# Windowed attention and a gated feed-forward: q and k of two batches loaded with two neighbouring tokens in a partition, and sorted apart by VectorE ahead of the transposes

## The chip, the cores and the metric

The kernel runs on one core of a Trainium2 chip. TensorE (PE in the profile) multiplies matrices out of the on-chip memory SBUF into the accumulators (PSUM); VectorE (DVE) and ScalarE (ACT) work on elements and empty PSUM; GpSimd (POOL) and SyncE (SP) issue most of the DMAs that move data between the device's memory and SBUF. The metric is the device time of one execution in microseconds (us); lower is better.

## The reference

q, k and v have 4 batches, 8 heads, 768 tokens and a head size of 64. A query attends to the first 4 tokens (the sinks) and to itself and the 127 tokens before it. What comes out, with the heads side by side (3072 rows of 512), goes through a feed-forward without a nonlinearity:

```python
scores = scale * np.matmul(q, k.transpose(0, 1, 3, 2))
keep = is_sink | in_window            # pos < 4, or 0 <= rel < 128
scores = np.where(keep, scores, -1000000000.0)
a = np.exp(scores - np.max(scores, axis=-1, keepdims=True))
a = a / (np.sum(a, axis=-1, keepdims=True) + 1e-09)
attn = np.matmul(a, v)                # then (4*768, 512)
h = (attn @ w1) * (attn @ w2) @ w3    # w1, w2: 512x1024, w3: 1024x1024
out = h @ w_out                       # 1024x512, float32
```

## The kernel before

Everything is computed in bf16 with fp32 accumulation. The tokens of a batch are 6 blocks `kb` of 128, or 3 pairs `t` of blocks.

**Weights.** `w3 @ w_out` is folded into one matrix `w3o` once: w3 is transposed on TensorE in pieces (`fold_w3`, tiles `tp3`, L407, which VectorE copies to `w3t`, L412) and multiplied with `w_out` (`fold_mm`, tiles `ph` and `pw`, L437). Nine 512 KB pieces of w3 and `w_out` come as fp32 from SyncE (L165), are parked in tiles that are not yet used, among them q's and k's of batch 1 (`kN_88`, `qN_84`, `kqT_96`), and are cast by VectorE and ScalarE (L417). The rest comes from GpSimd's queue, whose DMAs cast on the way.

**Attention.** `load_qkv` (L108 to 110) loads, for a block of 128 tokens, k, q and v in one DMA each: partition p holds token p of the block, and each of its 8 heads is a run of 64 elements. `transposes` (L208 to 216) then makes eight 128x128 transposes of the block's k and q on TensorE (L213) into one PSUM tile `tp`, and one VectorE copy (L215) brings it to `kqT`, in which tokens run along the free dimension. Batch 2 and 3 have part of their transposes done by DMA from SyncE instead (`XPOSE`). Scores of k against q (`sc`, L260 and L281; of the sinks `sp`, L242), the exponential on ScalarE (`ex`, L265 and L285), the mask on VectorE (`am`, L269 and L289), the product with v (`av`, L313 and L350), and the division by the row's sum on VectorE (`rec` and `xn`) follow; `xn` is transposed into `xT`.

**Feed-forward.** `gate` (L383 to 399) multiplies `xT` with w1 and w2 (`pg`, L390); ScalarE empties the one (L397) and VectorE multiplies the other with it (`ab`, L394). `project` (L447 to 462) multiplies `ab` with `w3o` (`po`, L451), ScalarE empties it, and SyncE stores it.

**What sets the order.** Each piece of work is a `task` with a priority, a list of stages (engine and a planned duration), what it comes after, the loads it needs and the PSUM ring it takes a buffer from. `service` and `landings` (L474 to 514) plan when each load arrives, from `order`, the list of GpSimd's DMAs. `plan` (L674) goes through time by these figures and picks the next task of each engine; `nudge` adds to priorities and `PACE` sets least distances between score tasks. The outcome is one fixed order of instructions for each engine: at run time an engine takes its instructions in that order, and one that waits for a semaphore holds up all behind it. Where the plan sees TensorE idle early on, it puts in `keep_busy` multiplications (`pz`, L468) that nothing uses. The planned duration of a transposes task is 0.45 on TensorE and 0.65 on VectorE (L576).

Of the kernel before, what the change touches and what calls it, by code (L numbers as in the profile page):

```python
# [21 lines left out]
def kernel(  # L22
# [13 lines left out]
    nc = tc.nc  # L36
    FP32 = mybir.dt.float32
    BF16 = mybir.dt.bfloat16
# [19 lines left out]
    X_XPOSE = ((1, 0), (1, 1), (1, 2), (2, 0), (2, 1), (2, 2), (3, 0), (3, 1), (3, 2))  # L58
    HALVED = ((3, 1), (3, 2), (3, 3))
    SPLIT = 6  # L60
    scale = 1.0 / float(D) ** 0.5

    const = ctx.enter_context(tc.tile_pool(name="const", bufs=1))
# [2 lines left out]
    work = ctx.enter_context(tc.tile_pool(name="work", bufs=3))  # L66
# [4 lines left out]
    ident = const.tile([P, P], BF16, name="ident")  # L71
# [28 lines left out]
    def rows(src, b, kb):  # L100
        return src[b, :, kb * P:(kb + 1) * P, :].rearrange("h p d -> p h d")

    def heads(ap):
        return ap.rearrange("p (h d) -> p h d", d=D)

    kqv = k, q, v

    def load_qkv(b, kb):  # L108
        for src, dst in zip(kqv, (heads(kN[b][:, kb, :]), heads(qN[b][:, kb, :]), vN[b][:, kb, :, 0:D])):
            nc.gpsimd.dma_start(out=dst, in_=rows(src, b, kb))  # L110

# [17 lines left out]
    def load(what, *i):  # L129
# [9 lines left out]
        else:  # L139
            for dst, src in ((w1_sb, moe_w1), (w2_sb, moe_w2)):  # L140
# [5 lines left out]
            ("w3", 3, 4, "dve")]  # L146
    hold = 5

    order = [("w3", 6, 8), ("qkv", 0, 0, 1), ("qkv", 0, 1, 2), ("w3", 5, 6), ("qkv", 0, 2, 3),
             ("qkv", 0, 3, 4), ("w12", 0, 1), ("w12", 1, 2), ("w12", 2, 3), ("w12", 3, 4), ("qkv", 0, 4, 5),  # L150
             ("qkv", 0, 5, 6), ("qkv", 1, 0, 6), ("qkv", 2, 0, 6), ("qkv", 3, 0, 6)]

    nudge = {("g", 0, 1, 5, 0): -300, ("g", 1, 0, 6, 1): 60, ("p", 3, 5, 256): -300, ("g", 2, 0, 3, 0): -300}

    def flat(tile_, names):
        return tile_[:].rearrange(f"p {names} -> p ({names})")
# [47 lines left out]
    for x in order:  # L204
        if x[0] != "qkv" or x[1] == 0:
            load(*x)

    def transposes(b, kb):  # L208

        tp = ps_mm.tile([P, 2, NP, P], BF16, tag="mm", name="tp")  # L210
        for i, src in enumerate((kN[b], qN[b])):
            for r in range(NP):
                nc.tensor.transpose(tp[:, i, r, :], src[:, kb, r * P:(r + 1) * P], ident)  # L213
        yield
        nc.vector.tensor_copy(kqT[b][:, :, :, kb * P:(kb + 1) * P], tp[:])  # L215
        yield

    def transposes_dma(src, dst, kb):
# [254 lines left out]

    def service(what, *i):  # L474
        if what == "qkv":
            return [(0.95 if i[0] == 0 else 0.87, 0.845 if 6 * i[0] + kb < 14 else 2.1, [(x, i[0], kb)])
                    for kb in range(i[1], i[2]) for x in "kqv"]
# [85 lines left out]
    for b in range(B):  # L563
        for t in range(NT):
            kbs = (2 * t, 2 * t + 1)
            qk = []
            war = [("av", b - 2, NP - 1, NT - 1)] if b >= 2 else []
            for kb in kbs:
                if (b, t) in XPOSE:
                    for n, src, dst in (("k", kN[b], kT[b]), ("q", qN[b], qT[b])):  # L570
                        qk.append(("td" + n, b, kb))
                        task(qk[-1], 1, transposes_dma(src, dst, kb), [("sp", 1.4), ("dma", 1.2)],
                             war, [(n, b, kb)])
                else:
                    qk.append(("tpk", b, kb))
                    task(qk[-1], 1, transposes(b, kb), [("pe", 0.45), ("dve", 0.65)],  # L576
                         war, [("k", b, kb), ("q", b, kb)], "mm")
            if t == 0:
                task(("sk", b), 0, sink_keys(b), [("dve", 0.2)], [("sc", b, 1, 0)])
                task(("sv", b), 2, sink_values(b), [("dve", 0.6)],  # L580
                     [("av", b - 1, 1, NT - 1)] if b else [], [("vc",)])
            else:
                if b not in SINKS:
                    task(("ss", b, t), -1, sink_scores(b, t, t + 1), [("pe", 0.12), ("act", 0.4)],
                         qk + [("sk", b)], ring="mm", started=[] if (b, t) in BLOCKS else [("sc", b, 1, t)])
                elif t == 1:
                    more = [(n, b, kb) for n in (("tdk", "tdq") if (b, 2) in XPOSE else ("tpk",)) for kb in (4, 5)]
                    task(("ss", b, 1), -1, sink_scores(b, 1, NT), [("pe", 0.225), ("act", 0.6)],
                         qk + more + [("sk", b)], ring="mm", started=[("sc", b, 1, 1)])
            if (b, t) in BLOCKS:  # L590
                parts = [(j, r0, r0 + 2, [2 * i + r0 // 2]) for i, j in enumerate(kbs) for r0 in (0, 2)]
                if t == 0:
                    parts = [(0, 0, NP, [0, 1])] + parts[2:]
                for u, (j, r0, r1, avs) in enumerate(parts):
                    lead, more = j in PAIRS and r0 == 0, j in PAIRS and r0 > 0
                    task(("sc", b, u, t), 0 if more else 4, block_scores(b, j, r0, r1),
                         [("pe", 0.23), ("act", 1.05), ("dve", 0.7)],
                         [("tpk", b, kb) for kb in (j - 1, j) if kb >= 0], ring="sc",
                         slots=2 if lead else 1, paced=not more,
                         started=([unit[-1][0]] if unit else [])  # L600
                         + (unit[-3 if lead else -4][1] if len(unit) > 3 else []))
# [12 lines left out]
            for r in range(NP):  # L614
                after = list(qk)
                if b >= 2 and t == 0:
                    after += [("g", b - 2, len(CHUNKS[b - 2]) - 1, dt, 1) for dt in range(KFF)]
                lead = r % 2 == 0
                task(("sc", b, r, t), 4 if lead else 0, scores(b, r, t),
                     [("pe", 0.17), ("act", 0.83), ("dve", 0.58)] if t == 0 else  # L620
                     [("pe", 0.225), ("act", 1.05), ("dve", 0.7)], after, ring="sc",
                     slots=2 if lead else 1, paced=lead,
                     started=([unit[-1][0]] if unit else []) + (unit[-3][1] if lead and len(unit) > 3 else []))
                task(("av", b, r, t), 3, values(b, r, t),
                     [("pe", 0.187 if t == 0 else 0.36), ("dve", 0.55)],
                     [("sc", b, r, t)] + ([("ss", b, 1 if b in SINKS else t), ("sv", b)] if t else []),
                     [("v", b, kb) for kb in kbs], "mm", last_av)
                last_av = [("av", b, r, t)]
                unit.append((("sc", b, r, t), last_av))
                if not lead and (b, t) not in X_XPOSE:  # L630
                    task(("xt", b, r - 1, t), 2.5, x_transposes(b, r - 1, t),
                         [("pe", 0.225), ("act", 0.6)],
                         [("av", b, r - 1, t), ("av", b, r, t)], [], "mm")
            if (b, t) in X_XPOSE:
                for i in range(2):
                    task(("xd", b, t, i), 1, x_transposes_dma(b, t, i), [("sp", 1.3), ("dma", 1.2)],
                         [("av", b, NP - 1, t)])
    gates = []
    for b in range(B):
# [26 lines left out]
    MARGIN = {"av": 0.3}  # L666

    YIELD = {"g": 0.0, "av": 0.0, "sc": 0.4, "tdk": 1.5, "tdq": 1.5}
    PACE = [[0, 0, 0], [0, 0, 0], [0, 0, 7.6], [8.9, 3, 5.4]]
    TURN, SHAPE = 0.095, {"sc": 1, "ss": 2}  # L670
    START, WARM_UNTIL = 1.2, 40.0
    BACKLOG = 1.6
# [158 lines left out]
```

## Time and profile before

| | us |
|---|---|
| median of 3 runs (lowest, highest) | 195.99 (195.43, 197.69) |
| span of the profiled execution, from its first to its last instruction | 193.9 |
| TensorE busy in the span | 186.7 |
| VectorE busy in the span | 114.7 |
| ScalarE busy in the span | 103.0 |
| 12 VectorE copies `kqT<-tp` (L215) | 8.3 |
| 24 loads each of k, q and v, median from issue to landing | 8.2 to 8.6 |

The span is the one time that the profile has of its execution; the median of the runs, which were not profiled, is 2.1 us more, which holds what lies ahead of the first instruction and behind the last as well as the difference between executions.

How to read it: busy time counts from an instruction's start to its end, and TensorE overlaps its multiplications, so that the time from one start to the next is less than the duration in a row. In a timeline a row has the start, the time from the first start to the last end, the engine, the line, and in brackets the idle time of that engine ahead of it with what ended it. An engine that idles costs time only where the engine that sets the end waits for it.

### The profile page before, as it was taken

To read this page: it belongs to the slowest core of one execution; us is meant where nothing else is said; L and a number is where in the kernel's file an instruction comes from. 1 tells how busy PE (TensorE), PEld (TensorE's weight loads), DVE (VectorE), ACT (ScalarE), POOL (GpSimd) and SP (SyncE) were. 2 spreads that over 40 slices of the span, in tenths; PEclk is the share of its full clock that TensorE was granted. 3 is DMA by queue.
4 is the path that set the end of the run, shared out by engine and by line. 5 is a ranking of instruction groups with operands and counts; after the bars stand their busy time and mean duration, and the time that the engine had idled before them with its cause. 6 is when DMAs were issued, how large, how long until landed. Compare 5 with 4: busy or idle time off the path is not lost.

```text
span 193.9 us, 4599 instructions
## 1 busy us (share of the span) xinstructions
PE 186.7 (96%) x1808; PEld 123.1 (63%) x1825; DVE 114.7 (59%) x277; ACT 103.0 (53%) x175; POOL 75.2 (39%) x102
## 2 busy tenths in 40 slices
PE   7899999999999999999999999999999999999994
PEld 2344556898867787588799556654666565655542
DVE  5554687856699887678785435660588564444100
ACT  4052289743766876575764627352884563333232
POOL 5189987688899863443155351000000000000000
PEclk9999999999999999999999999999999999999999
DMA  6999999999999999999999999999320432000144
GB/s 219 372 391 179 170 159 196 196 161 153 155 147 194 195 150 119 154 133 238 144 140 158 144 164 209 190 153 205 113 52 6 110 110 55 0 0 3 68 162 149
DMA packets 108021, 29.17 MB, mean 150 GB/s; under 512 B 98656, under 2 KB 103904, under 8 KB 108000
## 3 DMA queue, kind: packets, MB, share of 16 engines
q0 software_dynamic: 79520, 12.33, 90.4%
q1 hardware_dynamic: 28336, 16.49, 40.5%
q8 instruction: 14, 0.23, 0.5%
q10 hardware_dynamic: 144, 0.07, 0.1%
q14 instruction: 7, 0.06, 0.1%
HBM read 29.39 MB, written 6.29 MB: 184 GB/s over the span
## 4 chain that ended last, share of the span: by engine, by line
PE 88%; DMA 8%; SPq 1%; issue 1%; DVE 0%; POOL 0%; ACT 0%
PE pg L390 44%; PE po L451 21%; PE av L350 7%; PE sc L260 5%; DMA ab<-in_moe_w_out_dram 4%; DMA w_sb<-in_moe_w_dram 4%; PE tp L213 3%; PE pw L437 3%; PE av L313 1%; PE sc L281 1%; PE tp L407 1%; PE ph L437 1%; SPq L165 1%; PE sp L242 1%; PE xt L329 1%
## 5 line engine op out<-in xcount | busy, mean ns | idle before, releaser
L390 PE MATMUL pg<-xT,w_sb 128*128 128x256 bf16 (+1 forms) x640 | 90.8, 294 | 0.0
L390 PEld LDWEIGHTS <-w_sb 128*128 128x128 bf16 x640 | 59.8, 98 | 20.7 <-issue 1.7
L397 ACT COPY a_sb<-pg 128x256 f32<-128x256 f32 (+1 forms) x80 | 33.3, 416 | 37.4 <-PE pg L390 24.1
L394 DVE TENSOR_TENSOR ab<-a_sb,pg 128x256 bf16<-128x256 f32 (+1 forms) x80 | 37.6, 471 | 23.8 <-PE pg L390 21.2
L451 PE MATMUL po<-w3o,ab 128*128 128x512 bf16 (+2 forms) x196 | 42.7, 362 | 0.5
L265 ACT ACTIVATE ex<-sc 128x1024 bf16<-128x1024 f32 (+1 forms) x40 | 37.9, 963 | 5.3 <-PE sc L260 4.6
L269 DVE TENSOR_TENSOR am<-ex,maskt 128x1024 bf16<-128x1024 bf16 (+1 forms) x40 | 25.3, 646 | 12.8 <-ACT ex L265 12.8
L451 PEld LDWEIGHTS <-ab 128*128 128x128 bf16 x208 | 19.1, 98 | 19.7 <-issue 0.2
L455 ACT COPY w_sb<-po 128x512 f32<-128x512 f32 (+2 forms) x25 | 14.1, 564 | 26.2 <-PE po L451 24.1
L110 POOL DMA_DIRECT2D kN<-in_k_dram x24 | 21.6, 900 | 13.1 <-DMA qN<-in_q_dram 9.2
L110 POOL DMA_DIRECT2D qN<-in_q_dram x24 | 21.8, 909 | 11.9 <-DMA vN<-in_v_dram 7.7
L110 POOL DMA_DIRECT2D vN<-in_v_dram x24 | 21.4, 893 | 8.6 <-DMA kN<-in_k_dram 7.6
L357 DVE TENSOR_TENSOR xn<-av,rec 128x256 bf16<-128x256 f32 x40 | 17.0, 425 | 1.4
L350 PE MATMUL av<-vN,am 128*128 128x65 bf16 x296 | 16.9, 193 | 0.0
L350 PEld LDWEIGHTS <-am 128*128 128x128 bf16 x296 | 14.5, 97 | 2.3 <-issue 0.2
L354 DVE RECIPROCAL rec<-av 128x4 f32<-128x4 f32 x40 | 7.2, 180 | 12.3 <-PE av L350 12.2
L260 PE MATMUL sc<-kqT 64*128 64x128 bf16 (+1 forms) x216 | 11.6, 238 | 0.1
L350 PE MATMUL av<-vs,es 128*128 128x130 bf16 x56 | 11.1, 221 | 0.0
L285 ACT ACTIVATE ex<-sc 128x1024 bf16<-128x1024 f32 x7 | 7.1, 1045 | 5.3 <-PE sc L281 5.3
L260 PEld LDWEIGHTS <-kqT 64*128 64x128 bf16 x216 | 6.9, 94 | 4.0 <-issue 3.4
L215 DVE COPY kqT<-tp 128x1024 bf16<-128x1024 bf16 x12 | 8.3, 689 | 1.8 <-PE tp L213 1.7
L437 PE MATMUL ph<-wo_sb,w3t 128*128 128x512 bf16 x32 | 8.1, 379 | 0.4 <-DVE w3t L412 0.3
(70 smaller groups left out, 126.5 us busy)
## 6 DMA issues: line engine op xcount, KB each, us to landing
out_dram<-w_sb SPq DMA_DIRECT2D x20, 256.0 KB
kN<-in_k_dram POOLq DMA_DIRECT2D x24, 128.0 KB, 8.6
qN<-in_q_dram POOLq DMA_DIRECT2D x24, 128.0 KB, 8.2
vN<-in_v_dram POOLq DMA_DIRECT2D x24, 128.0 KB, 8.6
w_sb<-in_moe_w_dram POOLq DMA_DIRECT2D x9, 256.0 KB, 8.5
ab<-in_moe_w_dram SPq DMA_DIRECT2D x4, 512.0 KB
ab<-in_moe_w_out_dram SPq DMA_DIRECT2D x2, 512.0 KB
out_dram<-w_sb SPq DMA_DIRECT2D x7, 128.0 KB
```

The costliest lines, as they stand in the source:

```text
L110: nc.gpsimd.dma_start(out=dst, in_=rows(src, b, kb))
L260: nc.tensor.matmul(sc[:, e, c:c + n], kT[b][hp, r, kb * P:(kb + 1) * P], qT[b][hp, r, qb * P:qb * P + n], start=True, stop=True)
L265: nc.scalar.activation(ex[:, :, c0:], sc[:, :, c0:], ACTF.Exp, scale=scale)
L269: nc.vector.tensor_mul(am[:, :, c0:], ex[:, :, c0:], mk)
L350: nc.tensor.matmul(o, lhs, rhs, start=(n == 0), stop=(n == len(todo) - 1), skip_group_check=True)
L357: nc.vector.tensor_mul(xns[b, t][:, :, r, :, :], av[:, :, :, 0:D], rec[:].to_broadcast([P, 2, 2, D]))
L390: nc.tensor.matmul(pg[:], w_sb[:, kk, dt * P:(dt + 1) * P], xT[b][:, kk, tk], start=(kk == 0), stop=(kk == NP - 1))
L394: nc.vector.tensor_mul(ab[b][:, dt, tk], gate_a.pop((b, c, dt))[:], pg[:])
L397: nc.scalar.copy(a_sb[:], pg[:])
L437: nc.tensor.matmul(po, w3T[i][:, j, :], wo_sb[:, j, :], start=(j == 0), stop=(j == KFF - 1))
L451: nc.tensor.matmul(po[:], ab[b][:, kk, m * P:(m + 1) * P], w3o[:, kk, n0:n1], start=(kk == 0), stop=(kk == KFF - 1))
L455: (nc.vector.tensor_copy if n0 == DM // 2 else nc.scalar.copy)(o_sb, po[:])
```

## The change

For the batches in `WIDE` (0 and 1) k and q are loaded two blocks at a time (`load_pair`): partition p holds tokens 2p and 2p+1 of the pair of blocks, so that a run in the source is 128 elements (512 bytes of fp32) in place of 64, and a DMA has as many runs as before and twice the bytes. There are 12 such DMAs in place of 24. v is loaded as before.

The two tokens of a partition are neighbours there, head by head, while a transpose wants one token in a partition for all heads. So `part` makes a VectorE copy for each pair and each of k and q (12 in all), which brings the first tokens of all partitions to `pt[:, 0]` and the second ones to `pt[:, 1]`. The transposes read `pt`. A transposed block then holds every second token, so the copy out of PSUM to `kqT` writes every second element (a step of two in place of side by side); its planned duration stays at 0.65. Both blocks of a pair have to be transposed before scores of either can start.

In `order` the first k, q and v stand ahead of `w3[6:8]`, and `nudge` (from 4 entries to 37) and `PACE` are others.

```diff
+    WIDE = (0, 1)
...
+    def paired(x, b, t):
+        return x[b][:, 2 * t:2 * t + 2, :].rearrange("p k n -> p (k n)").rearrange("p (h i d) -> p h i d", i=2, d=D)
+
+    def load_pair(b, t):
+        for src, x in ((k, kN), (q, qN)):
+            nc.gpsimd.dma_start(out=paired(x, b, t).rearrange("p h i d -> p h (i d)"),
+                                in_=src[b, :, t * 256:(t + 1) * 256, :].rearrange("h (p i) d -> p h (i d)", i=2))
+        for kb in (2 * t, 2 * t + 1):
+            nc.gpsimd.dma_start(out=vN[b][:, kb, :, 0:D], in_=rows(v, b, kb))
...
-    order = [("w3", 6, 8), ("qkv", 0, 0, 1), ("qkv", 0, 1, 2), ("w3", 5, 6), ("qkv", 0, 2, 3),
-             ("qkv", 0, 3, 4), ("w12", 0, 1), ("w12", 1, 2), ("w12", 2, 3), ("w12", 3, 4), ("qkv", 0, 4, 5),
-             ("qkv", 0, 5, 6), ("qkv", 1, 0, 6), ("qkv", 2, 0, 6), ("qkv", 3, 0, 6)]
-
-    nudge = {("g", 0, 1, 5, 0): -300, ("g", 1, 0, 6, 1): 60, ("p", 3, 5, 256): -300, ("g", 2, 0, 3, 0): -300}
+    order = [("qkv", 0, 0, 2), ("w3", 6, 8), ("qkv", 0, 2, 4), ("w3", 5, 6), ("w12", 0, 1), ("w12", 1, 2),
+             ("w12", 2, 3), ("w12", 3, 4), ("qkv", 0, 4, 6), ("qkv", 1, 0, 6), ("qkv", 2, 0, 6), ("qkv", 3, 0, 6)]
+
+    nudge = {('g', 0, 1, 5, 0): -300, ('g', 1, 0, 6, 1): 60, ('p', 3, 5, 256): -300, ('av', 0, 1, 1): 3, ('g', 2, 1, 1,
...
+    def part(b, n, t):
+
+        parted[b, n, t] = work.tile([P, 2, DM], BF16, tag=f"pt{n}", bufs=1, name=f"pt{n}")
+        nc.vector.tensor_copy(parted[b, n, t][:].rearrange("p i (h d) -> p h i d", d=D), paired((kN, qN)[n], b, t))
+        yield
+
     def transposes(b, kb):
...
-        for i, src in enumerate((kN[b], qN[b])):
+        for i, src in enumerate((kN, qN)):
             for r in range(NP):
-                nc.tensor.transpose(tp[:, i, r, :], src[:, kb, r * P:(r + 1) * P], ident)
-        yield
-        nc.vector.tensor_copy(kqT[b][:, :, :, kb * P:(kb + 1) * P], tp[:])
+                rows_of = parted[b, i, kb // 2][:, kb % 2, :] if b in WIDE else src[b][:, kb, :]
+                nc.tensor.transpose(tp[:, i, r, :], rows_of[:, r * P:(r + 1) * P], ident)
+        yield
+        to = kqT[b][:, :, :, kb // 2 * 256:kb // 2 * 256 + 256].rearrange("p x r (n i) -> p x r n i", i=2)[:, :, :, :, kb % 2] \
+            if b in WIDE else kqT[b][:, :, :, kb * P:(kb + 1) * P]
+        nc.vector.tensor_copy(to, tp[:])
         yield
...
-    PACE = [[0, 0, 0], [0, 0, 0], [0, 0, 7.6], [8.9, 3, 5.4]]
+    PACE = [[0, 0.0, 0.0], [1, 2, 0], [2.0, 1.5, 7.6], [8.9, 4, 10.9]]
```

What it does to the fixed order shows at three places. First GpSimd's queue, from its first load on; `w_sb` stands for the weights, `kN_87`, `qN_83` and `vN_91` are k, q and v of batch 0. Before:

```order
L127 DMA w_sb<-in_moe_w_dram 128x2x1024
L132 MEMSET vN_91 128x48
L110 DMA kN_87<-in_k_dram 128x8x64
L110 DMA qN_83<-in_q_dram 128x8x64
L110 DMA vN_91<-in_v_dram 128x8x64
```

Now:

```order
L147 MEMSET vN_91 128x48
L114 DMA kN_87<-in_k_dram 128x8x128
L114 DMA qN_83<-in_q_dram 128x8x128
L117 DMA vN_91<-in_v_dram 128x8x64 x2
L142 DMA w_sb<-in_moe_w_dram 128x2x1024
```

The 512 KB of `w3[6:8]` went from the head of the queue to behind four loads, and the first k is now a load of two blocks.

Second VectorE around the first transposes. `w3t<-tp` are copies for the weights' fold, `kqT_95` is batch 0's transposed k and q, and `pt` is what the new copies write. Before, from the last cast of a parked weight:

```order
L417 CAST w_sb<-kqT_96 128x1024
L412 COPY w3t<-tp_302 128x512
L412 COPY w3t<-tp_307 128x512
L412 COPY w3t<-tp_314 128x512
L412 COPY w3t<-tp_326 128x512
L233 TENSOR_TENSOR vs_111<-vc,ones_s 128x8x64
L215 COPY kqT_95<-tp 128x8x128
```

Now, from the same cast:

```order
L449 CAST w_sb<-kqT_96 128x1024
L234 COPY pt_296<-kN_87 128x8x2x64
L444 COPY w3t<-tp_291 128x512
L444 COPY w3t<-tp_305 128x512
L234 COPY pt_315<-qN_83 128x8x2x64
L265 TENSOR_TENSOR vs_111<-vc,ones_s 128x8x64
L247 COPY kqT_95<-tp 128x8x128 x2
```

The copy `pt_296`, which waits for the first k to land, stands ahead of two copies for the fold, and the two copies to `kqT` follow each other.

Third VectorE at the last pair of blocks of batch 0, among the first gates (`ab_103`). Before:

```order
L394 TENSOR_TENSOR ab_103<-a_sb,pg 128x256 x4
L215 COPY kqT_95<-tp 128x8x128
L394 TENSOR_TENSOR ab_103<-a_sb,pg 128x256 x4
L215 COPY kqT_95<-tp 128x8x128
L394 TENSOR_TENSOR ab_103<-a_sb,pg 128x256 x2
```

Now:

```order
L426 TENSOR_TENSOR ab_103<-a_sb,pg 128x256
L234 COPY pt_783<-kN_87 128x8x2x64
L426 TENSOR_TENSOR ab_103<-a_sb,pg 128x256
L234 COPY pt_814<-qN_83 128x8x2x64
L426 TENSOR_TENSOR ab_103<-a_sb,pg 128x256 x2
L247 COPY kqT_95<-tp 128x8x128 x2
L426 TENSOR_TENSOR ab_103<-a_sb,pg 128x256 x2
```

Four gate products stood between the two copies to `kqT`; now the copies follow each other, with the two copies to `pt` a little ahead of them.

More of the change, by code (lines that the diff above doesn't have):

```diff
@@ L106 @@
     kqv = k, q, v
+    def paired(x, b, t):
[6 more added lines that the diff above has]
+            nc.gpsimd.dma_start(out=vN[b][:, kb, :, 0:D], in_=rows(v, b, kb))
     def load_qkv(b, kb):
+        if b in WIDE:
+            if kb % 2 == 0:
+                load_pair(b, kb // 2)
+            return
         for src, dst in zip(kqv, (heads(kN[b][:, kb, :]), heads(qN[b][:, kb, :]), vN[b][:, kb, :, 0:D])):
@@ L206 @@
             load(*x)
+    parted = {}
+    def part(b, n, t):
+        parted[b, n, t] = work.tile([P, 2, DM], BF16, tag=f"pt{n}", bufs=1, name=f"pt{n}")
+        nc.vector.tensor_copy(parted[b, n, t][:].rearrange("p i (h d) -> p h i d", d=D), paired((kN, qN)[n], b, t))
+        yield
     def transposes(b, kb):
         tp = ps_mm.tile([P, 2, NP, P], BF16, tag="mm", name="tp")
-        for i, src in enumerate((kN[b], qN[b])):
+        for i, src in enumerate((kN, qN)):
             for r in range(NP):
-                nc.tensor.transpose(tp[:, i, r, :], src[:, kb, r * P:(r + 1) * P], ident)
+                rows_of = parted[b, i, kb // 2][:, kb % 2, :] if b in WIDE else src[b][:, kb, :]
+                nc.tensor.transpose(tp[:, i, r, :], rows_of[:, r * P:(r + 1) * P], ident)
         yield
-        nc.vector.tensor_copy(kqT[b][:, :, :, kb * P:(kb + 1) * P], tp[:])
+        to = kqT[b][:, :, :, kb // 2 * 256:kb // 2 * 256 + 256].rearrange("p x r (n i) -> p x r n i", i=2)[:, :, :, :, kb % 2] \
+            if b in WIDE else kqT[b][:, :, :, kb * P:(kb + 1) * P]
+        nc.vector.tensor_copy(to, tp[:])
         yield
@@ L475, in service @@
         if what == "qkv":
+            if i[0] in WIDE:
+                return [x for t in range(i[1], i[2], 2) for x in
+                        [(0.9, 1.4, [(n, i[0], t), (n, i[0], t + 1)]) for n in "kq"]
+                        + [(0.9, 0.845, [("v", i[0], kb)]) for kb in (t, t + 1)]]
             return [(0.95 if i[0] == 0 else 0.87, 0.845 if 6 * i[0] + kb < 14 else 2.1, [(x, i[0], kb)])
@@ L567 @@
             war = [("av", b - 2, NP - 1, NT - 1)] if b >= 2 else []
+            if b in WIDE:
+                before = [("tpk", b - (t == 0), x) for x in (2 * (t - 1) % NB, (2 * t - 1) % NB)] if b or t else []
+                for n in range(2):
+                    task(("pt", b, n, t), 1, part(b, n, t), [("dve", 0.55)], before, [("kq"[n], b, 2 * t)])
             for kb in kbs:
@@ L576 @@
                     task(qk[-1], 1, transposes(b, kb), [("pe", 0.45), ("dve", 0.65)],
-                         war, [("k", b, kb), ("q", b, kb)], "mm")
+                         war + [("pt", b, n, t) for n in range(2) if b in WIDE],
+                         [] if b in WIDE else [("k", b, kb), ("q", b, kb)], "mm")
             if t == 0:
@@ L597 @@
                          [("pe", 0.23), ("act", 1.05), ("dve", 0.7)],
-                         [("tpk", b, kb) for kb in (j - 1, j) if kb >= 0], ring="sc",
+                         [("tpk", b, kb) for kb in (range((j - 1) // 2 * 2 if j else 0, j // 2 * 2 + 2) if b in WIDE else (j - 1, j))
+                          if kb >= 0], ring="sc",
                          slots=2 if lead else 1, paced=not more,
```

7 rows, old and new, of the table nudge are left out of this document.

## The prediction

> **What bounds the kernel now.** I read the busy shares first, then TensorE's idle time stage by stage, then what ended it.
>
> ```profile
> PE 186.7 (96%) x1808; PEld 123.1 (63%) x1825; DVE 114.7 (59%) x277; ACT 103.0 (53%) x175; POOL 75.2 (39%) x102
> ```
>
> The busy time by stretch (columns: stretch and length, then busy time and count of PE, weight loads, DVE, ACT, POOL):
>
> ```profile
> 10.00:20.00 10.00, 9.46 (x65) 4.89 (x67) 5.12 (x13) 3.72 (x4) 9.11 (x12) 1.00 1.44 274
> 20.00:65.00 45.00, 44.26 (x558) 33.18 (x563) 34.06 (x83) 29.16 (x49) 38.33 (x48) 1.00 2.10 171
> 65.00:110.00 45.00, 44.84 (x531) 35.43 (x531) 33.14 (x88) 29.18 (x55) 20.48 (x25) 1.00 1.85 156
> 110.00:180.00 70.00, 69.64 (x564) 40.82 (x568) 36.50 (x82) 34.48 (x59) 4.22 (x5) 1.00 0.71 98
> ```
>
> TensorE sets the end: between 10 and 180 us it idles 0.54 + 0.74 + 0.16 + 0.36 = 1.8 us in all. Its waits in the part that the change touches are these two (in total, times, longest):
>
> ```profile
> PE tp L407 <- DMA w_sb<-in_moe_w_dram: 0.4, 1, 0.4
> PE sc L281 <- DVE kqT L215: 0.4, 1, 0.4
> ```
>
> So there is little to win, and whatever makes TensorE wait is paid in full, since each engine's order is fixed. The multiplications are the same in number before and now (1808 run, 17 of them `pz` in both orders), so I count only waits.
>
> **The loads.** The chain of waits, GpSimd's timeline, the DMA issues of short windows (with us to landing), and the bytes by 40 slices of 4.85 us give the rate:
>
> ```profile
> 10.85 7.31 DMA w_sb<-in_moe_w_dram
> ...
> 24.19 0.77 POOL L113 DMA_DIRECT2D w_sb<-in_moe_w_dram  x1
> ...
> 31.48 0.91 POOL L110 DMA_DIRECT2D kN<-in_k_dram  x1
> ...
> w_sb<-in_moe_w_dram POOLq DMA_DIRECT2D x1, 256.0 KB, 7.0
> ...
> w_sb<-in_moe_w_dram POOLq DMA_DIRECT2D x1, 256.0 KB, 10.2
> ...
> GB/s 219 372 391 179 170 159 196 196 161 153 155 147 194 195 150 119 154 133 238 144 140 158 144 164 209 190 153 205 113 52 6 110 110 55 0 0 3 68 162 149
> ```
>
> The first of the eight DMAs of w1 and w2 (runs of 256 elements) landed at 24.19 + 7.0 = 31.2, and the last, issued just ahead of the k at 31.48, 10.2 after its issue, at about 41. The seventh and eighth slices (29 to 39 us) are theirs: 196 GB/s. The tenth (43.6 to 48.5 us) holds loads of q, k and v alone: 153 GB/s, so 131 KB take 0.86 us. A paired load has runs of 128, between the two, so its 262 KB take 1.34 to 1.71 us; I take 1.4, since doubling the run from 64 is the larger step. Twelve of them save 12 x (1.72 - 1.4) = 3.8 us of the load stream. TensorE waits for loads for 0.4 us only, so the saving as such is worth next to nothing, and what counts is when the first loads land.
>
> GpSimd's first load was issued at 10.85 and landed at 18.16. It was 512 KB; now it is the first k with 256 KB, so it lands no later than 18.2, and no earlier than 1.34 us before, 16.8. I take 17.5, the middle. q then lands a load later, at 18.9 to 19.2, and `w3[6:8]` behind it and two v at 18.16 + 2 x 1.34 (or 1.71) + 2 x 0.86 = 22.6 to 23.3.
>
> **The first wait moves.** VectorE's copy `pt_296` waits for k, and behind it in VectorE's order stands the copy `w3t<-tp_291` that TensorE's fold needs. The timeline before, TensorE then the rows with prices:
>
> ```profile
> 13.73 3.63 PE L437 MATMUL ph<-wo_sb,w3t 128*128 128x512 bf16 x16
> 17.20 0.61 PE L407 MATMUL tp<-ident,w_sb 128*128 128x128 bf16 x8
> ```
>
> ```profile
> 23.25 0.45 PE tp L213 x8
> ...
> 24.56 0.43 PE ph L437 x2
> ...
> 64.34 0.44 PE pg L390 x4
> ...
> 68.57 0.46 PE av L350 x10
> ```
>
> TensorE has those 16 and those 8 ahead of it now as well (four of the 8 in among the 16), so it comes to the fold's next piece at 17.20 + 0.45 = 17.65. VectorE's prices, by shape:
>
> ```profile
> L215 DVE COPY kqT<-tp 128x1024 bf16<-128x1024 bf16 x12 | 8.3, 689 | 1.8 <-PE tp L213 1.7
> L412 DVE COPY w3t<-tp 128x512 bf16<-128x512 bf16 x12 | 4.7, 420 | 5.4 <-PE tp L407 5.4
> L417 DVE CAST w_sb<-ab 128x1024 bf16<-128x1024 f32 x3 | 2.1, 694 | 2.7 <-DMA ab<-in_moe_w_dram 2.7
> L228 DVE COPY ksbd<-kqT 64x16 bf16<-64x16 bf16 x8 | 1.3, 163 | 0.1
> L394 DVE TENSOR_TENSOR ab<-a_sb,pg 128x256 bf16<-128x256 f32 x48 | 19.9, 417 | 9.7 <-PE pg L390 8.3 <-ACT a_sb L397 0.7 <-PE xt L329 0.4
> L394 DVE TENSOR_TENSOR ab<-a_sb,pg 128x384 bf16<-128x384 f32 x32 | 17.7, 552 | 14.2 <-PE pg L390 12.9 <-ACT ex L265 0.7
> L455 DVE COPY w_sb<-po 128x128 f32<-128x128 f32 x1 | 0.3, 292 | 1.6 <-PE po L451 1.6
> ```
>
> A copy to `pt` has 1024 elements from SBUF to SBUF in bf16, which before never does at this size. It costs more than 0.16 (L228, 16 elements) and no more than 0.69 (L417, the same count from twice the bytes). I take 0.69, the row of its size, less the 0.08 by which neighbouring copies overlap. [...]
>
> TensorE waits until 17.5 + 0.61 + 0.42 and the 0.06 from a copy's end to TensorE's start (below) = 18.6, so **0.95 us** (0 with k at 16.8 and the low price, 1.6 with the high ends). Queued behind `pt_296` are both fold copies, for which TensorE alone waits. The old wait for `w3[6:8]` goes, and so does the one of the scores, which the next part prices anew: **-0.8**. q's copy ends at 19.9 and is hidden by six fold multiplications (1.29 us) that bring TensorE from 18.6 to 19.9.
>
> **The copies out of PSUM are the largest term.** How transposes, copies and scores follow each other (the second row is VectorE's next copy, the third the scores that wait for the first):
>
> ```profile
> 21.35 0.68 DVE L215 COPY kqT<-tp 128x1024 bf16<-128x1024 bf16 x1
> 21.95 0.42 DVE L412 COPY w3t<-tp 128x512 bf16<-128x512 bf16 x1
> 22.09 0.40 PE L281 MATMUL sc<-kqT 64*128 64x128 bf16 x8 [0.37 <-DVE kqT L215]
> 23.09 0.39 PE L213 MATMUL tp<-ident,kN 128*128 128x128 bf16 x4
> 23.73 0.69 DVE L215 COPY kqT<-tp 128x1024 bf16<-128x1024 bf16 x1
> ```
>
> A copy can start 0.64 after its transposes (23.09 to 23.73), the next copy 0.08 before its end (21.95), and TensorE 0.06 after it (22.03 to 22.09). VectorE shows two rates: L412 to L215, 512 more elements in 0.27 us, 0.53 ns each; L394, 128 more in 0.135 us, 1.05 ns each. Now the copy writes every second 2-byte element, which no row does. The low bound is today's 0.69; the high one is L455's copy out of PSUM, 0.292, plus 896 x 1.05 ns = 1.23 us. The nearer row is a choice: in count and type it is L215, in the span that the writes cover (512 bytes for 128 elements) L455. I take **1.23**, because the fast rows all write side by side, and just that goes.
>
> [...]
>
> With transposes of a pair starting at S, TensorE is free at S + 0.90. The first copy runs from S + 0.64 to 1.87, the second to S + 3.02, and TensorE can go on at S + 3.08 (at 0.69: S + 1.99). What the new order puts between, pair by pair:
> - first: six fold multiplications, 1.29, until S + 2.19: wait 0.89.
> - second: 4 transposes (0.22), 4 fold (0.86), 8 `av` (0.37 by the row of 10), 4 transposes (0.22), until S + 2.57; VectorE has two `ksbd` copies (0.33) in between, S + 3.41: wait 0.84.
> - third: 12 `pg`, 1.31, of which the last four need the first copy's buffer (S + 1.93): 0.16, then 0.71 for the second: 0.87.
> - fourth (batch 1): 10 `av` (0.46), 4 `pg`, then 4 that need the first copy (0.13), then 4 that need the second (0.71): 0.84.
> - fifth and sixth: only the first copy stands ahead of what TensorE waits for, so the excess of one, 0.54 each.
>
> Sum **4.5 us**; at 0.69 each place comes out before TensorE gets there, so 0. With the first pair's wait, `w3[6:8]` is needed at 19.9 + 3.08 + 0.33 = 23.3, just as it lands, so that wait is covered (without it 0.2 to 0.9).
>
> The other ten `pt` copies are hidden by VectorE's idle time: in 20 to 65 us it has 45 - 34.06 = 10.94, plus the 4.5 by which the stretch gets longer; they and the twelve longer copies take 10 x 0.69 + 12 x 0.54 = 13.4. If that cover is gone, 13.4 - 10.94 = 2.5 us show. `nudge` and `PACE` reorder work that is the same in sum; behind 65 us TensorE idles 0.52 us until 180, so I put nothing there, up to 0.5 either way.
>
> **Sum:** 193.9 + 0.95 - 0.8 + 4.5 = 198.6 for the span, and, with the median of 195.99 standing 2.1 above the span of before, **200.7 us**.
>
> **Rivals.** (1) *VectorE writes every second element at the fast rate.* For it: L215 is its like in count and type, and no row of before speaks against it. Then 195.99 - 0.8 + 0.95 + 0.5 (`w3[6:8]`) = 196.6, with the low ends of load and `pt` 195.2: not slower. It decides at about 0.8 for the `kqT` copy, up to which the places above stay covered (the first: 0.64 + 2 x 0.8 - 0.08 + 0.06 = 2.2). (2) *VectorE becomes the bound* from 20 to 65 us, because its idle time falls where it has nothing to do: 2.5 more, 203.2. Against it: in the stretches of before its idle time is spread. (3) *Faster by more than 1%*, under 194.03: if all of the 1.8 us of idle time between 10 and 180 us went, it would be 194.2, so this takes shorter work as well; the profile has no room for it. (4) *The paired load takes as long as two* (1.71): k lands 0.3 later, 0.3 us more, inside the range.
>
> **How the numbers follow.** My forecast has 63% (198.5 to 202.5 by the ends of the first wait and some of the places being hidden), rival 2 has 9%, rival 1 has 26%, of which 5 parts below 194.03 with the re-ordering's help, and rival 3 proper 2%. That gives slower by over 1% 72%, within 1% 21%, faster 7%; 1% is about what a measurement of this kernel can tell from no change. The range has to reach into rival 1 to leave out no more than 2 in 10: 195.2 to 203.0; the likeliest case alone is 198.5 to 202.5.
>
> **What would show it.** The `kqT` copies of batches 0 and 1 at a mean of 1.2 us (0.69: rival 1); TensorE's waits for `kqT` at 0.7 to 1 us, three or four times, and one of about 1 us for `w3t`; TensorE's idle time from 20 to 65 us at 4 to 5 us in place of 0.74; VectorE busy by 6.5 + 12 x (0.16 to 0.69) more; batch 2's first load issued some 4 us sooner. It is wrong if the strided copy is fast, or if the order gives TensorE other work at these places than I read.

## The result and the profile after

The changed kernel takes **203.77 us** (median), the kernel before 196.12 beside it: a ratio of 1.0385, 95% interval 1.0341 to 1.043. It is slower, as forecast, but by 7.7 us and not 4.7, which is just above the top of the range, 203.0. One of its four executions was slow, with 206.91 us, and is left out of the ratio; the middle one of the other three took 203.48, so differences taken below from 203.77 would be 0.3 less by it. The profiled execution has a span of 201.7 us, 7.8 above that of before.

Busy shares and granted TensorE clock of the changed kernel (from its page), then the stretches of the prediction:

```profile
PE 190.9 (95%) x1825; PEld 124.5 (62%) x1825; DVE 126.7 (63%) x289; ACT 102.8 (51%) x175; POOL 64.7 (32%) x90
...
PEclk9999879999999999999999999999999999999999
```

```profile
10.00:20.00 10.00, 9.78 (x68) 4.91 (x66) 5.31 (x11) 3.48 (x4) 9.87 (x14) 1.00 1.51 266
20.00:65.00 45.00, 39.59 (x483) 29.60 (x482) 37.62 (x78) 25.40 (x43) 32.20 (x40) 0.96 1.93 176
65.00:110.00 45.00, 44.32 (x533) 33.36 (x531) 37.18 (x94) 29.46 (x53) 19.33 (x23) 1.00 1.83 164
110.00:180.00 70.00, 70.00 (x589) 41.93 (x587) 35.61 (x85) 34.70 (x61) 0.00 (x0) 1.00 0.48 91
```

The loss is where the prediction put it: TensorE idles 45 - 39.59 = 5.41 us from 20 to 65 us, before it was 0.74. From 65 to 110 us it idles 0.68 us (before 0.16), and behind that nothing is lost. But the granted clock is below 1 for a while (0.96 in the mean of 20 to 65 us); in the profile of before it is 1.00 up to 193 us and falls only in the last 0.9 (0.54 from 193 us on), 2 us behind TensorE's last multiplication. What TensorE waits for (in total, times, longest), and the groups of VectorE:

```profile
PE sc L313 <- DVE kqT L247: 2.7, 1, 2.7
...
PE sp L274 <- DVE rec L349: 1.2, 1, 1.2
PE sc L292 <- DVE kqT L247: 0.6, 1, 0.6
PE pg L422 <- DVE rec L386: 0.6, 1, 0.6
PE ph L469 <- DVE w3t L444: 0.3, 1, 0.3
```

```profile
L247 DVE COPY kqT<-tp 128x1024 bf16<-128x1024 bf16 x12 | 15.2, 1292 | 0.7 <-PE tp L243 0.7
L234 DVE COPY pt<-kN 128x1024 bf16<-128x1024 bf16 x6 | 3.2, 535 | 0.1
L234 DVE COPY pt<-qN 128x1024 bf16<-128x1024 bf16 x6 | 3.1, 522 | 0.0
```

The `kqT` copy went from 689 to 1292 ns. The wait at the first pair of blocks is 2.7 us, three times its forecast. VectorE and TensorE there:

```profile
16.16 0.58 DVE L234 COPY pt<-kN 128x1024 bf16<-128x1024 bf16 x1
16.66 0.41 DVE L444 COPY w3t<-tp 128x512 bf16<-128x512 bf16 x1
...
20.64 0.69 DVE L265 TENSOR_TENSOR vs<-vc,ones_s 128x512 bf16<-128x512 f32 x1 [2.13 <-issue]
21.25 2.46 DVE L247 COPY kqT<-tp 128x1024 bf16<-128x1024 bf16 x2
```

```profile
18.71 1.06 PE L243 MATMUL tp<-ident,pt 128*128 128x128 bf16 x16
...
20.03 1.03 PE L469 MATMUL ph<-wo_sb,w3t 128*128 128x512 bf16 x4
23.76 0.40 PE L313 MATMUL sc<-kqT 64*128 64x128 bf16 x8 [2.70 <-DVE kqT L247]
24.09 1.03 PE L439 MATMUL tp<-ident,w_sb 128*128 128x128 bf16 x8
```

The transposes start at 18.71, so the first copy could have started at 18.71 + 0.64 = 19.35. It started at 21.25. In front of it on VectorE stands `vs`, which makes the sink values out of `vc` and started only at 20.64. The chain of waits comes to it through the eight small loads of `vc`, which SyncE issues one after the other (from 5.5 to 15.0 us), and stays with the copies:

```profile
14.96 3.55 DMA vc<-in_v_dram
18.51 2.03 issue
21.25 2.46 DVE kqT L247 x2
```

The "issue" piece names no releaser; in five of the runs below the same instruction, in the same place of the order, waits for the DMA of `vc` by the profile. Then the clock, in three short stretches (the seventh number from the left is the granted clock):

```profile
20.00:24.00 4.00, 1.30 (x13) 0.52 (x11) 3.06 (x3) 1.60 (x2) 1.19 (x3) 1.00 1.63 185
24.00:27.50 3.50, 3.50 (x36) 2.01 (x30) 2.44 (x6) 2.05 (x2) 2.68 (x4) 0.51 1.79 182
27.50:30.00 2.50, 2.50 (x24) 1.36 (x22) 1.11 (x5) 1.21 (x2) 1.45 (x3) 1.00 1.45 195
```

Right behind the 2.7 us without a multiplication TensorE runs at half its clock for 3.5 us, that is up to 1.7 us of work not done.

### The profile page after: what moved, and what is told of

Same layout as the page of the kernel before. It is cut to its first block, busy times and chain, and to the rows that moved or that the text cites. A ratio compares the mean times of both kernels' runs of the same rounds, so it can differ in the third digit from the quotient of the medians.

```text
span 201.7 us, 4618 instructions
## 1 busy us (share of the span) xinstructions
PE 190.9 (95%) x1825; PEld 124.5 (62%) x1825; DVE 126.7 (63%) x289; ACT 102.8 (51%) x175; POOL 64.7 (32%) x90
## 3 DMA queue, kind: packets, MB, share of 16 engines
HBM read 29.39 MB, written 6.29 MB: 177 GB/s over the span
## 4 chain that ended last, share of the span: by engine, by line
PE 74%; DVE 13%; DMA 7%; issue 2%; SPq 2%; ACT 0%; DVEq 0%
PE pg L422 39%; PE po L483 18%; DVE kqT L247 7%; PE av L382 5%; DMA kqT<-in_moe_w_dram 5%; PE sc L292 4%; PE pw L469 2%; DMA vc<-in_v_dram 2%; SPq L186 2%; DVE am L301 1%; DVE xn L389 1%; PE sc L313 1%; PE tp L439 1%; PE av L345 1%; DVE pt L234 1%
## 5 line engine op out<-in xcount | busy, mean ns | idle before, releaser
L483 PE MATMUL po<-w3o,ab 128*128 128x512 bf16 (+2 forms) x208 | 43.6, 363 | 0.0
L382 PE MATMUL av<-vN,am 128*128 128x65 bf16 x296 | 16.8, 193 | 0.1
L247 DVE COPY kqT<-tp 128x1024 bf16<-128x1024 bf16 x12 | 15.2, 1292 | 0.7 <-PE tp L243 0.7
L125 POOL DMA_DIRECT2D qN<-in_q_dram x12 | 10.8, 898 | 8.3 <-DMA vN<-in_v_dram 7.4
L125 POOL DMA_DIRECT2D kN<-in_k_dram x12 | 10.6, 887 | 5.5 <-DMA qN<-in_q_dram 5.4
```

The source lines that it names most:

```text
L247: nc.vector.tensor_copy(to, tp[:])
L382: nc.tensor.matmul(o, lhs, rhs, start=(n == 0), stop=(n == len(todo) - 1), skip_group_check=True)
L483: nc.tensor.matmul(po[:], ab[b][:, kk, m * P:(m + 1) * P], w3o[:, kk, n0:n1], start=(kk == 0), stop=(kk == KFF - 1))
```

## The experiments

The theories. **T1**: the rate of the strided copy sets the loss at every place. **T2**: `vs` holds the first two copies back. **T3**: the long wait lets the clock fall, which costs on its own. Rivals: it is not the copy's rate but that a pair's scores wait for two copies; the new order and pacing numbers; the `pt` copies. In the kernels that keep the change's structure every engine takes the instructions that stay in the change's order, unless it is said otherwise. Ratios are to the kernel before, run beside them (medians 195.73 to 196.44).

**Copies side by side.**

```diff
-        to = kqT[b][:, :, :, kb // 2 * 256:kb // 2 * 256 + 256].rearrange("p x r (n i) -> p x r n i", i=2)[:, :, :, :, kb % 2] \
-            if b in WIDE else kqT[b][:, :, :, kb * P:(kb + 1) * P]
+        to = kqT[b][:, :, :, kb * P:(kb + 1) * P]
```

> The two kqT copies of a pair write 128 tokens side by side each, as before the change, and not every second token; nothing else is altered, and every engine's order stays. Left out is the interleaving: keys and queries of batches 0 and 1 stand in a wrong token order, so the scores are of other pairs of tokens. Theory 1 (the strided copy sets what is lost after the first place): the twelve copies fall from 1.29 us to about 0.69; at the first place 1.1 us goes, at the five later ones the 1.2, 0.9, 1.06 and 1.5 us that the two traces put there: 203.8 - 5.8 = 198.0 us; 196.3 if the shorter idle time also keeps TensorE's clock up. Theory 2 alone (the late sink values and the clock drop behind them cost most): only the first place moves, about 202.5. Rival (the copies are hidden; order, pacing numbers and pt copies cost the time): within 0.5 us of 203.8.

Measured: 196.78 us, ratio 1.0019 (0.9989 to 1.0048); a copy takes 686 ns, the clock stays at 1.00:

```profile
L247 DVE COPY kqT<-tp 128x1024 bf16<-128x1024 bf16 x12 | 8.0, 686 | 1.2 <-PE tp L243 1.1
```

```profile
PE tp L439 <- DMA w_sb<-in_moe_w_dram: 0.7, 1, 0.7
PE sc L313 <- DVE kqT L247: 0.2, 1, 0.2
```

Nearly the whole loss is gone, 7.0 of 7.7 us. `vs` still stands in front and still waits for `vc` here (1.4 us), which with fast copies no longer shows: the first wait is 0.2. The wait for `w3[6:8]`, which slow copies covered, is back. But this edit does two things: the copy is faster, and the first scores need only the first of the two copies.

**Both waited for, at the fast rate**, and **one waited for, at the slow rate**. The first swaps the halves so that the block that is needed first is copied last; the second writes side by side and reads PSUM with the step.

```diff
+        at = kb ^ 1 if b in WIDE else kb
+        to = kqT[b][:, :, :, at * P:(at + 1) * P]
```

> The two copies of a pair write side by side at the fast rate, but the first one made goes to the second half and the second to the first half, so that the first scores of a pair wait for both copies, as in the change; in the side-by-side run they needed only the first. Token order is left out as there. Theory A (the rate of the copy is the cause: 1.29 against 0.69 us): at the first place 0.69 us more than the side-by-side run's, elsewhere a little, about 197.7 us. Theory B (that a pair's scores wait for two copies and not for one costs most): 201 us or more, though each copy takes 0.69 us.

```diff
+        to = kqT[b][:, :, :, kb * P:(kb + 1) * P]
+        x, y = (to.rearrange("p x r (i n) -> p (x r) i n", i=2), tp[:].rearrange("p x r (n i) -> p (x r) i n", i=2)) if b in WIDE else (to, tp[:])
+        nc.vector.tensor_copy(x, y)
```

> The copies write side by side, so the first scores need one copy alone, but each reads its 128 columns from PSUM with a step of two elements, even ones first. Token order is left out. If the step slows a copy on the reading side as on the writing side, a copy takes about 1.29 us. Then by theory A the time is near the change's: 201.5 us or more (1.2 us less at the first place, and the clock may stay up); by theory B (waiting for both is what costs) 198 us or less. If a step on the reading side costs nothing, a copy takes 0.69 us and the time is the side-by-side run's 196.8.

Measured: 197.10 us (1.0048, 1.0014 to 1.0082) and 201.10 us (1.0255, 1.0202 to 1.0308). The copy and the first waits of the slow one:

```profile
L247 DVE COPY kqT<-tp 128x1024 bf16<-128x1024 bf16 x12 | 14.4, 1218 | 1.2 <-PE tp L243 1.2
```

```profile
PE sc L313 <- DVE kqT L247: 1.2, 1, 1.2
PE sp L274 <- DVE kqT L247: 1.1, 1, 1.1
```

| us | one copy waited for | both |
|---|---|---|
| copy at 0.69 | 196.8 | 197.1 |
| copy at 1.2 to 1.3 | 201.1 | 203.8 |

The rate alone costs 4.3 us, waiting for both alone 0.3, the two together 7.0. So the rate is the cause (theory A of the expectations), and waiting for both copies is not (theory B). The extra 2.4 belong to the pairing of the two: with both, the wait at the first place is 2.7 and not 1.2 us, and only then does the clock fall in the profiles. A small part of the 2.4 can be the copy's own time, 1292 ns in the change and 1218 with the step in the read.

**Sink values that need no load.**

```diff
-        nc.vector.tensor_mul(vs[b][:, :, 0:D], vc[:, b:b + 1, :].to_broadcast([P, H, D]),
+        nc.vector.tensor_mul(vs[b][:, :, 0:D], (vc[:, b:b + 1, :] if b else vz[:, 0:1, :]).to_broadcast([P, H, D]),
```

> The sink values of batch 0 are made from a zeroed tile and no longer from vc, so VectorE needn't wait for the eight vc loads ahead of the first kqT copies; each engine's order stays, one small memset on VectorE is added at the start. Left out are batch 0's sink values. Theory 2 (vs waits for vc and holds the first two kqT copies back): TensorE's first wait for kqT falls from 2.7 us to about 0.9, and with it the half clock from 24 to 27.5 us goes: 203.8 - 1.8 - 1.7 = 200.3 us. If the wait goes but the clock falls all the same: 202.0. Theory 1 alone (the strided copies cost everything, also at the first place): about 203.5, with the first wait still over 2 us.

Measured: 201.26 us, ratio 1.0257 (1.0201 to 1.0313), clock 1.00 throughout. VectorE, then TensorE:

```profile
19.39 0.69 DVE L265 TENSOR_TENSOR vs<-vz,ones_s 128x512 bf16<-128x512 f32 x1
20.70 2.48 DVE L247 COPY kqT<-tp 128x1024 bf16<-128x1024 bf16 x2 [0.62 <-PE tp L243]
```

```profile
20.06 1.06 PE L243 MATMUL tp<-ident,pt 128*128 128x128 bf16 x16
...
23.24 0.40 PE L313 MATMUL sc<-kqT 64*128 64x128 bf16 x8 [0.83 <-DVE kqT L247]
```

With `vs` out of the way the first copy starts 20.70 - 20.06 = 0.64 after its transposes, and TensorE waits 0.83 us: the prediction's rule and its 0.89. T2 holds. The time falls by 2.5 us and not 3.5: k landed later in this execution (the transposes start at 20.06, in the changed kernel's at 18.71), so the scores start only 0.5 us sooner.

**Both edits**, the side-by-side copy and the zeroed tile:

```diff
+        to = kqT[b][:, :, :, kb * P:(kb + 1) * P]
...
+        nc.vector.tensor_mul(vs[b][:, :, 0:D], (vc[:, b:b + 1, :] if b else vz[:, 0:1, :]).to_broadcast([P, H, D]),
```

> The first two edits together: kqT written side by side and batch 0's sink values from a zeroed tile (the same two things are left out), each engine's order kept. If the strided copies, the late sink values and the clock drop are all of it, what is left is the change with pt copies at no cost and loads that are shorter: 203.8 - 5.0 (copies: 1.1 less at the first place, of which the wait has 0.9 left, and 4.7 at the later ones) - 1.8 - 1.7 = about 195.5 us, at or a little under the kernel before. Rival (order, pacing numbers, pt copies cost something of their own): 198 us or more.

Measured: 196.96 us, ratio 1.0026 (0.9993 to 1.006). That is the side-by-side run's time, 1.5 above what was expected of it: I had added up effects that are not independent. With fast copies it makes no difference whether `vs` is late.

**Idle multiplications in the gap.**

```diff
+        sc = ps_sc.tile([P, 2, r1 - r0, len(kbs), P], FP32, tag="sc", name="sc"); [nc.tensor.matmul(sc[:, 0].rearrange("p r s q -> p (r s q)"), idle[:, 0:P], idle[:, 0:512], start=True, stop=True) for _ in range(12 if (b, j) == (0, 0) else 0)]
```

> Twelve idle matmuls (128x512, of zeros) stand on TensorE ahead of the first score matmuls, where it waits 2.7 us for kqT; all else keeps its order, nothing is left out. Theory 3 (the 2.7 us without a matmul let the granted clock fall to a half from 24.1 to 27.5 us, which costs 1.7 us): the clock stays up and the time falls to about 202.1 us, though the wait for kqT ends no sooner. Rival (the half clock comes of something else, or that stretch is bound by VectorE anyway): 203.8 +- 0.4, or up to 1 us more if the idle matmuls outlast the wait.

Measured: 202.66 us, ratio 1.0311 (1.027 to 1.0351). TensorE at the gap, and the stretch that had the half clock:

```profile
21.76 2.75 PE L308 MATMUL sc<-ksbd 128*128 128x512 bf16 x12
24.45 0.40 PE L313 MATMUL sc<-kqT 64*128 64x128 bf16 x8
...
29.39 1.06 PE L243 MATMUL tp<-ident,pt 128*128 128x128 bf16 x16
```

```profile
24.00:27.50 3.50, 3.34 (x47) 2.00 (x47) 2.65 (x7) 2.58 (x3) 1.99 (x4) 1.00 1.95 178
```

The scores start later than in the changed kernel's profile (24.45 against 23.76), the clock stays at 1.00, and the time is 1.1 us lower. T3 holds: with the gap filled the clock stays up. Its price in the profiles is 1.5 us: from these scores to the second pair's transposes TensorE takes 30.16 - 23.76 = 6.40 us in the changed kernel and 29.39 - 24.45 = 4.94 here, for the same multiplications. In the times it is less sure. Two other executions of the changed kernel had mean clocks of 0.999 and 0.990 and took 203.21 and 204.06 us, so the drop is not in every execution, and loads land at times that differ by as much (k's first copy to `pt` starts at 16.16 us in the changed kernel's profile, at 17.45 in this one). Nor is it shown that only this gap brings it: one execution in ten of each of three runs with fast copies (both edits, both waited for, loads without sorting) has a mean clock of 0.991, too, and took 1.7 to 2.2 us more than that run's median. Those three were not profiled.

**The loads without any sorting**, and **the new numbers without the change**.

```diff
-        nc.vector.tensor_copy(parted[b, n, t][:].rearrange("p i (h d) -> p h i d", d=D), paired((kN, qN)[n], b, t))
+        pass
...
-                rows_of = parted[b, i, kb // 2][:, kb % 2, :] if b in WIDE else src[b][:, kb, :]
+                rows_of = src[b][:, kb, :]
...
+        to = kqT[b][:, :, :, kb * P:(kb + 1) * P]
```

> The side-by-side kernel with its twelve pt copies taken out too: TensorE's transposes read the paired tile as it lies. What is left of the change is the paired loads and the new order and pacing; the sorting of tokens is left out altogether. If the pt copies (5.8 us of VectorE in all) lie beside other work: 196.5 +- 0.5 us, the same as with them. If they stand on the way to the transposes: down by up to the 0.95 us that the prediction put on the first one, 195.8. If the shorter loads buy TensorE anything, the time falls below the kernel before, 195.5 or less; by the reading of the trace (nothing in batches 0 and 1 but the first waits hangs on a load) it doesn't.

```diff
-    WIDE = (0, 1)
+    WIDE = ()
```

> The kernel before (single loads, no pt, side-by-side copies) with the change's order of loads, its nudges and its pacing numbers; nothing is left out. If order and pacing cost nothing of their own: 196.3 +- 1 us, the kernel before's; the one difference at the start is that w3[6:8] is loaded after two blocks of q, k and v and not ahead of them (0.4 us either way). Rival (the rearranged order is what slows the change): 198 us or more.

Measured: 196.66 us (1.004, 1.0003 to 1.0076) and 199.71 us (1.0193, 1.0143 to 1.0244). So, where the copies to `kqT` are fast, the twelve `pt` copies cost 0.1 us (against the side-by-side run), that is nothing that can be told apart. Paired loads with the new order, free of any sorting, are no faster than the kernel before. The second result contradicts what I expected: the new order with single loads is 3.3 us slower than the kernel before.

```profile
PE sc L292 <- DMA kqT<-qN: 1.0, 1, 1.0
PE tp L439 <- DVE w_sb L449: 1.0, 3, 0.4
PE tp L243 <- DMA qN<-in_q_dram: 0.8, 1, 0.8
PE tp L439 <- DMA w_sb<-in_moe_w_dram: 0.8, 1, 0.8
```

There q of the first block and then `w3[6:8]` are late, and in batch 2 a transpose made by DMA. My reading, which no run tests, is that these numbers fit the shorter stream of paired loads and cost with single ones. The planner also lays out another order for single loads, so this run doesn't price the numbers inside the changed kernel. That the order by itself slows the changed kernel is ruled out by the 196.7 and 196.8 us of the runs that have that order and paired loads.

**The slow copy in the kernel before.** Its copy reads PSUM with the step, and nothing else changes:

```diff
-        nc.vector.tensor_copy(kqT[b][:, :, :, kb * P:(kb + 1) * P], tp[:])
+        y = tp[:].rearrange("p x r (n i) -> p (x r) i n", i=2)
+        nc.vector.tensor_copy(kqT[b][:, :, :, kb * P:(kb + 1) * P].rearrange("p x r (i n) -> p (x r) i n", i=2), y)
```

> The kernel before with one thing altered: its twelve kqT copies read their 128 columns from PSUM with a step of two elements and write them side by side (token order within a block is left out); loads, order and pacing are those of the kernel before. In the slow-one run this made a copy 1.22 us. If the slow copy alone is the cause, wherever it stands, it costs here what it cost there, 201.1 - 196.8 = 4.3 us: 200.7 +- 0.7, near the 4.5 us that the prediction put on six places. If it hurts only in the change's order (where pt copies and w3t copies stand close to it on VectorE), 198 us or less.

Measured: 199.22 us, ratio 1.0196 (1.0156 to 1.0235).

```profile
L216 DVE COPY kqT<-tp 128x1024 bf16<-128x1024 bf16 x12 | 14.6, 1220 | 0.8 <-PE tp L213 0.8
```

The slow copy alone costs 3.1 to 4.6 us in an order that was made for the fast one, which can't be told from the 4.3 that it cost in the change's order; my 200.7 was too high by 1.5. It hurts in both orders.

**Sharing the copy with ScalarE**, as a way to keep the change. The first also has `vs` behind the first two blocks; both have orders of their own.

```diff
+        if b in WIDE:
+            nc.vector.tensor_copy(to[:, 0], tp[:, 0])
+            yield
+            nc.scalar.copy(to[:, 1], tp[:, 1])
```

> The whole computation, nothing left out: VectorE copies k's half of each kqT block with every second token, ScalarE q's half at the same time, and the sink values of batch 0 come behind the first two blocks on VectorE; the planner is told of both. If the rate of the strided copy is the cause, halving what one engine copies brings each block to about 0.65 us again, and the time to about 197.5 (198.5 if ScalarE's half is late behind exponentials, which stand ahead of it in its queue). If ScalarE's queue is the worse place, 201 us or more.

```diff
-        nc.vector.tensor_copy(to, tp[:])
+        (nc.scalar.copy if b in WIDE else nc.vector.tensor_copy)(to, tp[:])
```

> The whole computation, nothing left out: the twelve strided kqT copies stand on ScalarE and not on VectorE. ScalarE is busy for half of the span and took 0.6 us for 512 elements of a PSUM copy and 1.05 for 1024. If a step on the writing side costs ScalarE nothing, a copy takes about 1.05 us, and the time is between the side-by-side run's and the change's, 199 to 201 us, since the copies then stand between exponentials that the scores' successors need. If a copy takes 1.3 us or more there, 203 us or more.

Measured: 203.57 us (1.0397, 1.0362 to 1.0432) and 200.24 us (1.021, 1.0147 to 1.0273; its four executions took 198.8 to 202.1). The first is as slow as its last condition had it, the second fits neither of its cases: the copy took 1.31 us there, and the time is not 203. The copy's rows, half on ScalarE and then all of it:

```profile
L250 ACT COPY kqT<-tp 128x512 bf16<-128x512 bf16 x12 | 8.6, 738 | 5.9 <-DVE kqT L248 4.5 <-PE sc L297 1.1 <-DVE xn L394 0.4
```

```profile
L247 ACT COPY kqT<-tp 128x1024 bf16<-128x1024 bf16 x12 | 15.2, 1312 | 2.8 <-PE tp L243 2.8
```

On ScalarE the strided copy takes no less than on VectorE (1312 ns), and yet the kernel is 3.5 us faster than the change: TensorE's waits for it there are 0.6 and 0.3 us. Halving it did not help: TensorE's longest waits in that run are for transposes by DMA (`pg <- xT`, 1.9 us in all; 1.8 in the other run), in orders that are not the change's. Which part of either time is the order and which the copy stays open. Neither beats the kernel before, and no run in this direction did: even without any sorting the paired loads still stand at 196.7.

## Why the prediction was right or wrong

- **That TensorE's waits decide, and the saved load stream buys nothing:** right. Paired loads without sorting gave 196.66 against 196.44.
- **The strided copy falls into the slow rate (1.23 us taken):** right, 1.29 measured; of the two rows the choice of L455 as the nearer was the right one. Rival 1 is dead. Rival 2's time, 203.2, lies near the measured one, but not by its mechanism: VectorE still idles 7.4 us from 20 to 65 us, and what was lost sits at the places below. A step slows the copy on either side: with it in the write it takes 1292 ns, in the read 1218, in neither 686.
- **The first pair, 0.89:** this is the step that failed. It measured 2.70 of idle time, or 2.87 as the prediction counts, from 20.03 + 4 x 0.215 = 20.89 on, when TensorE's four fold multiplications are through. The prediction read "a copy can start 0.64 after its transposes" as if only the transposes stood ahead of it. But VectorE's order has `vs` between `pt_315` and the two copies; the row stands in the second excerpt of the order above, and the trace of before shows what it waits for:

```profile
20.74 0.69 DVE L233 TENSOR_TENSOR vs<-vc,ones_s 128x512 bf16<-128x512 f32 x1 [0.58 <-DMA vc<-in_v_dram]
```

  Before, the first block's transposes ended close to that, so `vs` was nearly free. The change brings k sooner but not `vc`. So the copies, which had become the path, waited 1.90 us (19.35 to 21.25) for a load that they don't need. In the run whose `vs` needs no load the wait was 0.83.
- **No term for the clock:** missing. Behind a wait of 2.7 us it was halved for 3.5 us; behind waits of 0.8 to 1.2 us in three runs it was not. It cost 1.5 us in the profiles, 1.1 by the times of the run that filled the gap.
- **The later places, 0.84 + 0.87 + 0.84 + 2 x 0.54 = 3.6:** right in kind, an eighth short. TensorE in the changed kernel and then in the side-by-side run, whose order is the same, from the second pair's transposes to the gates behind the sixth's:

```profile
30.16 1.06 PE L243 MATMUL tp<-ident,pt 128*128 128x128 bf16 x16
...
33.99 0.29 PE L274 MATMUL sp<-kqT,ksbd 128*32 128x256 bf16 x4 [1.16 <-DVE rec L349]
...
76.81 1.91 PE L422 MATMUL pg<-xT,w_sb 128*128 128x256 bf16 x16
```

```profile
27.36 1.06 PE L243 MATMUL tp<-ident,pt 128*128 128x128 bf16 x16
...
69.92 1.91 PE L422 MATMUL pg<-xT,w_sb 128*128 128x256 bf16 x16
```

  That is 46.65 us against 42.56, so these places cost 4.1. A copy took 0.06 more than I took, and other VectorE work stood in front; at the second place it was an `am`:

```profile
30.49 0.68 DVE L321 TENSOR_TENSOR am<-ex,maskt 128x1024 bf16<-128x1024 bf16 x1
31.09 1.29 DVE L247 COPY kqT<-tp 128x1024 bf16<-128x1024 bf16 x1
...
32.64 1.29 DVE L247 COPY kqT<-tp 128x1024 bf16<-128x1024 bf16 x1
```

  The first copy starts at 31.09 and not at 30.16 + 0.64 = 30.80. The profile names `rec` as what ended TensorE's wait there, but `sp` reads both blocks of the pair: the second copy ended at 33.93, and `sp` starts 0.06 behind it, the distance that the prediction used.
- **The first wait, 0.95:** it did not come. The 0.3 for `w3t` in the list of waits lies at 7.6 us, ahead of the first copy to `pt`. k landed before my earliest 16.8, for its copy started at 16.16; the fold copy behind it ended at 17.07, and TensorE came to the piece that needs it only at 17.41, straight from other work:

```profile
17.19 0.39 PE L439 MATMUL tp<-ident,w_sb 128*128 128x128 bf16 x4
17.41 0.59 PE L469 MATMUL ph<-wo_sb,w3t 128*128 128x512 bf16 x2
```

  In the two runs whose `vs` reads a zeroed tile k's copy started at 17.2 and 17.5, and the wait was 0.5. The `pt` copy took 0.53 on average (0.41 to 0.90), not 0.69.
- **The old waits, -0.8:** right; the one for `w3[6:8]` is covered by the slow copies, as the prediction had it, and returns with fast ones.

Put together: the old waits -0.8, the first wait 0, the first pair 2.87 as the prediction counts, the clock 1.5 and the later places 4.1 make 7.7, against 7.8 in the span. The terms come from several executions and loads land at other times in each, so the closeness of the two is in part luck.

## What to carry to other kernels

Before pricing a copy "so long after its producer", read the row that stands in front of it in its engine's order, and what that row waits for: an instruction that was harmless behind a slow load becomes the path when the load gets faster. A copy that re-sorts 2-byte elements with a step of two took 1.8 to 1.9 times as long as a side-by-side one here; a change that wants bigger DMA runs should be charged for that copy wherever the bound engine waits for it, and should first show that it waits for loads at all. Effects that meet at one wait don't add up: measure them alone and together.

## What the runs showed of the hardware

- A step of two costs VectorE nearly the same in the PSUM read (1218 ns) as in the SBUF write (1292 ns), against 686 ns for 128x1024 bf16 side by side; ScalarE took 1312 ns for the strided write.
- In the profiled execution of the changed kernel the granted clock fell to a half for 3.5 us right behind a gap of 2.7 us on TensorE at 24 us of the span. Behind gaps of up to 1.8 us (for `xT`, with the copies on ScalarE) it stayed at 1.00, and so it did where twelve multiplications of zeros filled the gap.
